# Output weights in 7168-byte runs, re-laid results and a one-row last load in a decode attention kernel

## The chip, the cores and the metric

One core of a Trainium2 chip. The core has a matrix engine (TensorE, PE in the profile), a vector engine (VectorE, DVE), a scalar engine (ScalarE, ACT), GpSimd (POOL) and SyncE (SP), which here only issues transfers. Sixteen DMA engines bring data from HBM to SBUF. Matmuls write to PSUM. The metric is the device time of one execution in microseconds (us); the profile's span runs from the first to the last instruction and is about 2 us shorter.

## The reference

One decode step of a block with attention and a dense part side by side, in bf16, for B = 2 rows of D = 448:

```python
xn = layernorm(x)
# A: 16 query heads, 8 KV heads (rep = 2), Dh = 256, the last W = 4096 keys of 32768
q = xn @ wq                                   # [2, 448] @ [448, 4096]
scores = q . k[:, :, Sk-W:, :] * Dh**-0.5
o = softmax(scores) @ v[:, :, Sk-W:, :]
a = o.reshape(2, 4096) @ wo                   # wo is [4096, 448]
# B: mish MLP
h = xn @ w1 + b1                              # F = 1792
b = (h * tanh(softplus(h))) @ w2
out = x + a + b
```

What has to be read is 2 x 8 x 4096 x 256 keys and as many values in bf16 (67.1 MB), and 3.67 MB each of wq and wo, and 1.6 MB each of w1 and w2: 77.66 MB in all.

## The kernel before

**Tiling.** The eight KV heads are worked off in U = 4 units. Unit u takes heads u and u + 4 of both batch rows, so J = 4 streams of 4096 keys. A unit's keys come in four loads of 2 MB (`load_k(u, r)`, L90, 16 KB per partition) and its values in four of 2 MB (`load_v(u, g)`, L96). Keys sit in a pool of 3 buffers, values in a ring of 4 (L67, L68). The query weights and w1 pass through the values' ring, w2 through a key buffer.

**One unit** (loop at L511). VectorE turns the keys of each load (`turns`, L498, two transposes at L243). When all four are turned, TensorE makes the scores in two halves (`scores`, L305), ScalarE the exponentials, VectorE turns them back (L333), and `weigh` (L340) sums them. Then `values` (L357) multiplies each tile of V; `gather` (L376) copies the result to SBUF and folds it by fp32 products with the masks `sel`, and `finish` (L409) divides by the sums. It leaves `oT`: the unit's attention output with the head dimension on the partitions, partition p holding rows 2p and 2p + 1 of each head's 256.

**Output product.** `load_wo(u)` (L105) brings the unit's part of wo, the 512 rows of each of its two KV heads (two query heads of 256), laid like `oT`: two rows of 448 to a partition, 1792 bytes per run, two loads of 448 KB. `mix` (L421) multiplies; `add_rows` (L221) splits the 448 output columns into G = 4 groups of 112 and puts each in another quarter of the PSUM tile `acc`, four matmuls for each row set. `mix(u - 1)` stands after `weigh(u)` in the unit loop. `acc` starts with x itself (L210 to L219) and takes all sums of attention and of the dense part.

**The end.** The last unit's fourth value tile is handled by `values_fixed` (L395), which works straight into the folded result, after `gather`. Then `finish`, `mix(3)`, and `dense_out` (L490) for the three loads of w2: all seven rows of the first half, five rows of the second, two rows of the second (`w2_parts`, L477). VectorE and ScalarE then copy `acc` into the result, and one store ends the kernel.

**Order.** The program is scheduled by hand: each engine works off its instructions in the order in which they are written, and SyncE issues all large loads in the written order. In a unit u below 3 that is V(u, 0) to V(u, 3), K(u + 1, 0) to K(u + 1, 2), wo(u), K(u + 1, 3); in the last unit wo(3), V, then w2. A load waits at SyncE until its buffer is free, and whatever is written after it waits behind it.

**PSUM.** Eight banks: two for scores, one each for the value products, the folded result, the sums and `acc`, and two (`ps_m`, L79) that rotate through the small products of the first stage (`xr_ps`, `q_ps`, `qt_ps`, `qr_ps`, `h_ps`).

Of the kernel before, what the change touches and what calls it, by code (L numbers as in the profile page):

```python
# [11 lines left out]
BF16 = mybir.dt.bfloat16  # L12
FP32 = mybir.dt.float32
PSUM = bass.MemoryType.PSUM
# [3 lines left out]
def kernel(  # L18
# [13 lines left out]
    nc = tc.nc  # L32
    P = 128
    G = 4
# [3 lines left out]
    Bsz, Sq, D = A_x.shape  # L38
    _, Hkv, Sk, Dh = A_k_cache.shape
    HqDh = A_wq.shape[1]  # L40
    Hq = HqDh // Dh
    rep = Hq // Hkv
# [3 lines left out]
    KU = J // Bsz  # L46
    U = Hkv // KU
# [11 lines left out]
    NI = F2 // P  # L59
    DG = D // G  # L60
# [11 lines left out]
    consts = ctx.enter_context(tc.tile_pool(name="consts", bufs=1))  # L72
    small = ctx.enter_context(tc.tile_pool(name="small", bufs=2))
# [2 lines left out]
    ps_o = ctx.enter_context(tc.tile_pool(name="ps_o", bufs=1, space=PSUM))  # L76
    ps_den = ctx.enter_context(tc.tile_pool(name="ps_den", bufs=1, space=PSUM))
    ps_a = ctx.enter_context(tc.tile_pool(name="ps_a", bufs=1, space=PSUM))
    ps_m = ctx.enter_context(tc.tile_pool(name="ps_m", bufs=2, space=PSUM))  # L79

    KE = T * Dh
    kview = A_k_cache.rearrange("b (k u) s d -> u (b k) s d", u=U)
# [5 lines left out]
    k_t, v_t, wo_t = {}, {}, {}  # L88

    def load_k(u, r):  # L90
        t = k_pool.tile([P, KE], BF16, tag="k", name="k")
        src = kview[u][:, s0:, :].rearrange("j (c t) d -> c j (t d)", c=C)
        nc.sync.dma_start(out=t[:], in_=src[:, :, r * KE : (r + 1) * KE])  # L93
        k_t[u, r] = t

    def load_v(u, g, lo=0, hi=T):  # L96
        if lo == 0:
            v_t[u, g] = ring("v")
        t = v_t[u, g]
        src = vview[u][:, s0:, :].rearrange("j (g x t) d -> g x j (t d)", g=G, x=C)  # L100
        nc.sync.dma_start(  # L101
            out=t[:, lo * Dh : hi * Dh], in_=src[g, :, :, lo * Dh : hi * Dh]
        )

    def load_wo(u):  # L105
        w = wo_pool.tile([P, KU, rep, 2 * D], BF16, tag="wo", name="wo")
        for k2 in range(KU):
            r0 = (u + U * k2) * rep * Dh
            nc.sync.dma_start(  # L109
                out=w[:, k2, :, :],  # L110
                in_=A_wo[r0 : r0 + rep * Dh, :].rearrange("(h p c) d -> p h (c d)", h=rep, p=P),
            )
        wo_t[u] = w

    x_bf = consts.tile([Bsz, D], BF16)
# [8 lines left out]
    for lo, hi in ((0, 4), (4, NS)):  # L124
# [5 lines left out]
    ident = consts.tile([P, P], BF16)  # L130
# [2 lines left out]
    nc.gpsimd.memset(qd[:], 0.0)  # L133
    ones = consts.tile([P, P], BF16)
    nc.gpsimd.memset(ones[:], 1.0)
    eps_t = consts.tile([Bsz, 1], FP32)
    nc.vector.memset(eps_t[:], 1e-5)

# [6 lines left out]
        out=rstd[:], in_=mv[:, 1:2], func=ACT.Sqrt, bias=eps_t[:], scale=1.0  # L145
# [4 lines left out]
        out=xn_bf[:],  # L150
# [8 lines left out]
        out=parm[:], in_=ident[:].rearrange("p (a o) -> p o a", o=2), axis=AXIS.X, op=ALU.add  # L159
# [3 lines left out]
        out=jm[:],  # L163
        in_=ident[:].rearrange("p (a j h) -> p j a h", j=J, h=rep),
# [4 lines left out]
        out=jm[:], in0=jm[:], scalar1=-1.0, scalar2=29952.0, op0=ALU.add, op1=ALU.mult  # L169
# [3 lines left out]
        out=mneg[:], in_=jm[:].unsqueeze(1).to_broadcast([P, TH * 8, J])  # L173
    )
    sel = consts.tile([P, 2, NQ], FP32)
    for x in range(2):
        for w in range(4):
# [4 lines left out]
            else:  # L182
                nc.vector.tensor_tensor(
                    out=sel[:, x, :], in0=sel[:, x, :], in1=src, op=ALU.add
                )

    xr_ps = ps_m.tile([P, NS, Bsz], BF16, tag="m", name="xr_ps")
    xn_v = xn_bf[:].rearrange("b (a k) -> b a k", k=NS)
    for s in range(NS):
        r = s // 2  # L190
        step = 3 + s % 2
        xrow = consts.tile([Bsz, P // 2, 2], BF16, name=f"xrow{s}")
        nc.vector.tensor_copy(out=xrow[:], in_=xn_v[:, :, r : r + step + 1 : step])  # L193
        nc.tensor.transpose(  # L194
            xr_ps[:, s, :], xrow[:].rearrange("b a o -> b (a o)"), ident[0:Bsz, 0:Bsz]
        )
    xs = consts.tile([P, NS, 32], BF16)
    nc.gpsimd.memset(xs[:], 0.0)
    for odd in range(2):
        for half in range(2):  # L200
            o = (half + odd) % 2
            nc.vector.tensor_scalar(
                out=xs[:, odd::2, half * Bsz : (half + 1) * Bsz],
# [3 lines left out]
                op0=ALU.mult,  # L207
            )

    acc = ps_a.tile([P, DG], FP32)  # L210
    for g in range(G):
        nc.tensor.matmul(
            acc[32 * g : 32 * (g + 1), :],
            lhsT=ident[0:Bsz, 0:32],
            rhs=x_bf[:, g * DG : (g + 1) * DG],
            start=True,
            stop=False,
            skip_group_check=True,
        )  # L219

    def add_rows(lhsT, rows, stop=False):  # L221
        for g in range(G):
            nc.tensor.matmul(  # L223
                acc[32 * g : 32 * g + Bsz, :],
                lhsT=lhsT,
                rhs=rows[:, g * DG : (g + 1) * DG],
                start=False,
                stop=stop,
                skip_group_check=True,
            )  # L230
# [20 lines left out]
    for n in range(2):  # L251
        for e in range(2):
            o = n * 64 + e
            sp = consts.tile([P, G, 32], BF16, name=f"sp{n}{e}")
            nc.gpsimd.tensor_copy(
                out=sp[:],
                in_=ident[:, o : o + 63 : 2].unsqueeze(1).to_broadcast([P, G, 32]),
# [47 lines left out]
    def scores(u, i):  # L305
        sc = ps_sc.tile([P, TH, 32], FP32, tag="sc", name="sc")
        nc.tensor.matmul(  # L307
            sc[:].rearrange("p t m -> p (t m)"),
            lhsT=ident[:],
            rhs=mneg[:].rearrange("p a j -> p (a j)"),  # L310
            start=True,
            stop=False,
            skip_group_check=True,
        )
        for n in range(NB):
            for e in range(2):
                for w in range(4):
                    nc.tensor.matmul(  # L318
                        sc[32 * w : 32 * (w + 1), :, :],
                        lhsT=qd[:, u, 2 * n + e, :, :].rearrange("p g q -> p (g q)"),  # L320
                        rhs=ktm[i][:, n, e, :, 32 * w : 32 * (w + 1)],
                        start=False,
                        stop=(n == NB - 1 and e == 1),
                        skip_group_check=True,
                    )
        ex = small.tile([P, TH, 32], BF16, tag="ex", name="ex")
        nc.scalar.activation(  # L327
            out=ex[:].rearrange("p t m -> p (t m)"),
            in_=sc[:].rearrange("p t m -> p (t m)"),
            func=ACT.Exp,  # L330
            scale=scale,
        )
        nc.vector.transpose(  # L333
            out=p_t[i][:].rearrange("p g t q -> p t g q"),
            in_=ex[:].rearrange("p t (g q) -> p t g q", g=G),
        )

    state = {}
# [70 lines left out]
    def finish(u):  # L409
# [8 lines left out]
        )  # L418
        state["oT", u] = oT

    def mix(u):  # L421
        oT, w = state.pop(("oT", u)), wo_t.pop(u)
        for k2 in range(KU):
            for h in range(rep):
                for c in range(2):
                    add_rows(oT[:, c, k2 * rep + h, :], w[:, k2, h, c * D : (c + 1) * D])
# [47 lines left out]
        nc.vector.tensor_tensor(out=t_sb[:], in0=t_sb[:], in1=den[:], op=ALU.mult)  # L474
        nc.vector.tensor_tensor(out=act_bf[:], in0=h_sb[:], in1=t_sb[:], op=ALU.mult)

    w2_parts = ((0, 0, NI), (1, 0, 5), (1, 5, NI))  # L477

    def load_w2(part):
        if part == 0:  # L480
            state["w2"] = k_pool.tile([P, KE], BF16, tag="k", name="w2")
        k, lo, hi = w2_parts[part]
        w2_in = B_w2.flatten().rearrange("(k p e) -> k p e", k=2, p=P)
        at = k * NI * D
        nc.sync.dma_start(
            out=state["w2"][:, at + lo * D : at + hi * D],
            in_=w2_in[k, :, lo * D : hi * D],
        )

    def dense_out(part):  # L490
        k, lo, hi = w2_parts[part]
        for i in range(lo, hi):
            at = (k * NI + i) * D
            add_rows(
                act_bf[:, i, k, :], state["w2"][:, at : at + D], stop=(k == 1 and i == NI - 1)
            )

    def turns(u, r):  # L498
        for i in range(NH):
            turn(u, r, i)  # L500
# [10 lines left out]
    for u in range(U):  # L511
        last = u == U - 1
        if last:
            load_wo(u)
        load_v(u, 0)
        load_v(u, 1)
        load_v(u, 2)
        if last:
            load_v(u, 3, 0, 24)
            load_v(u, 3, 24, T)  # L520
            for part in range(3):
                load_w2(part)
        else:
            load_v(u, 3)
            load_k(u + 1, 0)
            load_k(u + 1, 1)
            load_k(u + 1, 2)
            load_wo(u)
            load_k(u + 1, 3)
        scores(u, 0)  # L530
        scores(u, 1)
        weigh(u)
        if u > 0:
            mix(u - 1)
        for g in range(G - 1):
            values(u, g)
        if not last:
            values(u, G - 1)
            turns(u + 1, 0)
            turns(u + 1, 1)  # L540
            gather(u)
            finish(u)
            turns(u + 1, 2)
            turns(u + 1, 3)
    u = U - 1
    gather(u, last=False)
    values_fixed(u, G - 1, 0, 24)
    values_fixed(u, G - 1, 24, T)
    finish(u)
    mix(u)  # L550
    for part in range(3):
        dense_out(part)

    res = consts.tile([Bsz, D], BF16)
# [38 lines left out]
```

The softmax here doesn't subtract the row's maximum and nothing guards it: scores larger than these inputs give would overflow.

## Time and profile before

| | |
|---|---|
| time, median of 3 | 193.05 us (192.83 to 193.07) |
| span of the profiled execution | 191.1 us |
| bytes moved | 77.80 MB, 77.66 of them on SyncE's queue |
| DVE busy | 90.7 us (47%) |
| PE busy | 69.5 us (36%), weight loads 33.6 |
| ACT busy, POOL busy | 11.3 us, 2.9 us |
| wo loads | 8 of 448 KB |
| w2 loads | 784 KB, 560 KB, 224 KB |

The busy shares are averages over the whole span. The slices cut the span into 40 equal parts: a digit is the busy share of one part in tenths (9 is 90% or more), "DMA" is the mean over the sixteen DMA engines, and "GB/s" is what they moved. The queue list gives packets, megabytes and the share of sixteen engines' span. The chain follows the work that ended last back from the end. In a line of the timeline the columns are start, length, engine, line, operation, output<-inputs, shapes and count, and in brackets the idle time before it with what ended it; consecutive instructions of one kind are merged. Matmul lengths are modelled and overlap.

### The profile page before, as it was taken

How to read it: one execution, taken by the hardware profiler on the slowest of the kernel's cores; microseconds unless marked ns; L12 is line 12 of the kernel's file. 1: busy time of each engine (PE TensorE's matmuls, PEld its weight loads, DVE VectorE, ACT ScalarE, POOL GpSimd, SP SyncE). 2: the span in 40 equal slices, each digit the busy share in tenths (PEclk: the TensorE clock that was granted, in tenths of full speed). 3: DMA queues.
4: the chain of work that ended last, by engine and by line, in shares of the span. 5: the costliest groups of instructions: out<-in, count | busy, mean ns of one | idle time of the engine just before them, and what ended most of it. 6: DMA issues, size and time to landing. Idle time of an engine off the chain costs nothing.

```text
span 191.1 us, 2051 instructions
## 1 busy us (share of the span) xinstructions
PE 69.5 (36%) x892; PEld 33.6 (18%) x892; DVE 90.7 (47%) x96; ACT 11.3 (6%) x19; POOL 2.9 (2%) x13
## 2 busy tenths in 40 slices
PE   0201525197236000097334000395262000674492
PEld 0100115032104000033113000132031000222191
DVE  4887066583001998543004995823007994731001
ACT  3000030011001000011000000010010000020101
POOL 6000000000000000000000000000000000000000
PEclk9999999999955555559955555579855555599655
DMA  5999999999999999999999999999999999999980
GB/s 216 408 419 423 434 421 449 415 429 425 435 432 422 425 404 424 435 435 422 418 429 432 435 408 415 429 425 432 432 429 418 415 421 404 436 418 425 414 351 19
DMA packets 8081, 77.80 MB, mean 407 GB/s; under 512 B 1028, under 2 KB 3208, under 8 KB 3592
## 3 DMA queue, kind: packets, MB, share of 16 engines
q1 hardware_dynamic: 7796, 77.66, 96.7%
q8 instruction: 7, 0.11, 0.2%
q10 hardware_dynamic: 276, 0.01, 0.1%
q14 instruction: 2, 0.02, 0.0%
HBM read 77.67 MB, written 0.00 MB: 406 GB/s over the span
## 4 chain that ended last, share of the span: by engine, by line
DMA 86%; DVE 7%; SPq 2%; PE 2%; issue 0%; DVEq 0%
DMA k<-in_A_k_cache_dram 53%; DMA w<-in_B_w_dram 27%; DVE kt L243 7%; DMA wo<-in_A_wo_dram 7%; PE h_ps L443 1%; SPq L93 1%; SPq L126 1%; PE acc L223 0%; SPq L101 0%; DVEq L588 0%; DVE res L559 0%; SPq L109 0%
## 5 line engine op out<-in xcount | busy, mean ns | idle before, releaser
L243 DVE STREAM_TRANSPOSE kt<-k 128x2048 f32<-128x2048 f32 x32 | 72.1, 2291 | 55.4 <-DMA k<-in_A_k_cache_dram 55.4
L318 PE MATMUL sc<-kt,qd 128*32 128x512 bf16 x256 | 23.2, 519 | 62.2 <-DVE kt L243 62.2
L365 PE MATMUL pv<-v,p 128*32 128x512 bf16 x240 | 19.2, 456 | 23.1 <-DMA v<-in_A_v_cache_dram 23.1
L318 PEld LDWEIGHTS <-qd 128*32 128x32 bf16 x256 | 8.6, 117 | 74.6 <-issue 72.4
L365 PEld LDWEIGHTS <-p 128*32 128x32 bf16 x240 | 7.0, 106 | 33.5 <-issue 29.9
L333 DVE STREAM_TRANSPOSE p<-ex 128x512 bf16<-128x512 bf16 x8 | 5.7, 711 | 14.5 <-ACT ex L327 14.5
L327 ACT ACTIVATE ex<-sc 128x512 bf16<-128x512 f32 x8 | 4.8, 598 | 85.4 <-PE sc L318 85.4
L385 PE MATMUL o<-sel,vs 128*128 128x8 f32 x32 | 7.5, 364 | 2.9 <-ACT vs L379 2.9
L385 PEld LDWEIGHTS o<-sel,vs 128*128 128x128 f32 x32 | 7.1, 325 | 6.5 <-ACT vs L379 6.5
L265 PE MATMUL q_ps<-wq,xs 128*32 128x512 bf16 x28 | 3.4, 623 | 12.5 <-DMA wq<-in_A_wq_dram 12.5
L412 DVE TENSOR_TENSOR oT<-o,rec 128x16 bf16<-128x16 f32 x4 | 0.6, 145 | 12.2 <-PE o L400 12.2
L379 ACT COPY vs<-pv 128x512 f32<-128x512 f32 x4 | 2.3, 586 | 48.2 <-PE pv L365 48.2
L343 PE MATMUL dn<-p,ones 128*128 128x512 bf16 x8 | 3.1, 383 | 4.5 <-DVE p L333 4.5
L443 PE MATMUL h_ps<-xs,w 128*128 128x4 bf16 x49 | 2.8, 193 | 5.1 <-DMA w<-in_B_w_dram 5.1
L307 PE MATMUL sc<-mneg,ident 128*128 128x512 bf16 x8 | 4.6, 571 | 0.0
L282 DVE COPY qT<-qt_ps 128x16 bf16<-128x16 bf16 x4 | 0.4, 168 | 6.9 <-PE qt_ps L277 6.9
L351 DVE TENSOR_REDUCE rec<-dn 128x8 f32<-128x512 f32 x4 | 2.8, 692 | 1.9 <-PE dn L343 1.9
L443 PEld LDWEIGHTS <-w 128*128 128x128 bf16 x49 | 2.7, 152 | 5.2 <-DMA w<-in_B_w_dram 5.2
L265 PEld LDWEIGHTS <-xs 128*32 128x32 bf16 x28 | 1.1, 125 | 14.0 <-issue 14.0
L194 PE MATMUL xr_ps<-ident,xrow 2*128 2x2 bf16 x7 | 1.0, 181 | 6.5 <-DVE xrow L193 6.5
L223 PEld LDWEIGHTS <-oT 128*2 128x2 bf16 x128 | 1.8, 91 | 5.5 <-issue 5.1
L223 PE MATMUL acc<-wo,oT 128*2 128x112 bf16 x128 | 2.6, 232 | 0.3 <-DVE oT L412 0.3
(51 smaller groups left out, 28.8 us busy)
## 6 DMA issues: line engine op xcount, KB each, us to landing
k<-in_A_k_cache_dram SPq DMA_DIRECT2D x16, 2048.0 KB, 27.1
v<-in_A_v_cache_dram SPq DMA_DIRECT2D x15, 2048.0 KB, 23.6
wo<-in_A_wo_dram SPq DMA_DIRECT2D x8, 448.0 KB, 30.5
wq<-in_A_wq_dram SPq DMA_DIRECT2D x1, 2048.0 KB, 16.3
w<-in_B_w_dram SPq DMA_DIRECT2D x1, 1568.0 KB, 26.9
wq<-in_A_wq_dram SPq DMA_DIRECT2D x1, 1536.0 KB, 19.3
v<-in_A_v_cache_dram SPq DMA_DIRECT2D x1, 1536.0 KB, 26.8
w<-in_B_w_dram SPq DMA_DIRECT2D x1, 784.0 KB, 23.9
```

The lines of the kernel that those rows point to most:

```text
L223: nc.tensor.matmul(acc[32 * g : 32 * g + Bsz, :], lhsT=lhsT, rhs=rows[:, g * DG : (g + 1) * DG], start=False, stop=stop, skip_group_check= ...
L243: nc.vector.transpose(out=kt[i][:, :, :, r, :], in_=t[:, i * w : (i + 1) * w].bitcast(FP32).rearrange("p (a c j) -> p a c j", c=P // (R * ...
L265: nc.tensor.matmul(q_ps[32 * u : 32 * (u + 1), :], lhsT=xs[:, s, :], rhs=wq_t[s][:, u * 512 : (u + 1) * 512], start=(s == 0), stop=(s == N ...
L307: nc.tensor.matmul(sc[:].rearrange("p t m -> p (t m)"), lhsT=ident[:], rhs=mneg[:].rearrange("p a j -> p (a j)"), start=True, stop=False, ...
L318: nc.tensor.matmul(sc[32 * w : 32 * (w + 1), :, :], lhsT=qd[:, u, 2 * n + e, :, :].rearrange("p g q -> p (g q)"), rhs=ktm[i][:, n, e, :, 3 ...
L327: nc.scalar.activation(out=ex[:].rearrange("p t m -> p (t m)"), in_=sc[:].rearrange("p t m -> p (t m)"), func=ACT.Exp, scale=scale,)
L333: nc.vector.transpose(out=p_t[i][:].rearrange("p g t q -> p t g q"), in_=ex[:].rearrange("p t (g q) -> p t g q", g=G),)
L343: nc.tensor.matmul(dn[:].rearrange("p a q -> p (a q)"), lhsT=ones[:], rhs=p_t[i][:].rearrange("p g t q -> p (g t q)"), start=(i == 0), sto ...
L351: nc.vector.tensor_reduce(out=rec[:], in_=dn[:].rearrange("p a q -> p q a"), axis=AXIS.X, op=ALU.add)
L365: nc.tensor.matmul(pv[32 * w : 32 * (w + 1), :, :].rearrange("p x d -> p (x d)"), lhsT=p_t[a // 4][:, g, 4 * (a % 4) : 4 * (a % 4) + 4, :] ...
L385: nc.tensor.matmul(po[:, c, :], lhsT=sb[:, x, c::2], rhs=sel[:, x, :], start=(x == 0 and c == 0), stop=(last and x == 1), skip_group_check ...
L443: nc.tensor.matmul(h_ps[:, i, :, :].rearrange("p k b -> p (k b)"), lhsT=w1_v[:, s, i, :], rhs=xs[:, s, 0 : 2 * Bsz], start=(s == 0), stop= ...
```

## The change

**Three units' output weights in longer runs.** For units 0 to 2, eight consecutive rows of wo go to one partition: 8 x 448 x 2 = 7168 bytes in one run, 128 runs, one load of 896 KB. Row y * 8 + i of KV head k lies at partition (y, k), place i. That is no longer the layout of `oT`.

**Re-laid results.** So `relay` brings `oT` into the new layout by products with one-hot masks (`hot`, made at the start on GpSimd): 16 small matmuls pick for each partition its rows, and ScalarE copies the result to `ox`.

**Mixed at full width, ahead of the next scores.** `mix_early` multiplies `ox` by the weights in eight matmuls of all 448 columns into a new PSUM tile `early`, in place of 32 matmuls of 112 columns into `acc`. Both stand ahead of `scores` of the next unit instead of after `weigh`. `early` starts with x. In the last unit `carry` copies `early` to SBUF and puts it into `acc` by four fp32 products with a 2 x 2 identity; the last unit itself is mixed as before. `early` has its own bank, so `ps_m` falls from two to one. The seven small rows `xrow` move into buffers that the exponentials use later.

**Last load one row.** The second half of w2 comes in 4 + 2 + 1 rows instead of 5 + 2.

```diff
-    ps_m = ctx.enter_context(tc.tile_pool(name="ps_m", bufs=2, space=PSUM))
+    ps_e = ctx.enter_context(tc.tile_pool(name="ps_e", bufs=1, space=PSUM))
+    ps_m = ctx.enter_context(tc.tile_pool(name="ps_m", bufs=1, space=PSUM))
...
     def load_wo(u):
         w = wo_pool.tile([P, KU, rep, 2 * D], BF16, tag="wo", name="wo")
-        for k2 in range(KU):
+        if u < U - 1:
+            nc.sync.dma_start(
+                out=w[:].rearrange("p k h e -> p (k h e)"),
+                in_=A_wo.rearrange("(k u y i) d -> u y k (i d)", k=KU, u=U, i=8)[u],
+            )
+        for k2 in range(KU if u == U - 1 else 0):
...
+    id2 = consts.tile([Bsz, Bsz], FP32)
+    nc.vector.tensor_copy(out=id2[:], in_=ident[0:Bsz, 0:Bsz])
+    hot = consts.tile([P, KU, 4, 32, KU], BF16)
+    nc.gpsimd.memset(hot[:], 0.0)
+    for k in range(KU):
+        nc.gpsimd.tensor_copy(
+            out=hot[:, k, :, :, k], in_=ident[:].rearrange("p (q y) -> p y q", y=4)
+        )
...
+    early = ps_e.tile([Bsz, D], FP32)
+    nc.tensor.matmul(
+        early[:], lhsT=ident[0:Bsz, 0:Bsz], rhs=x_bf[:], start=True, stop=False
+    )
     acc = ps_a.tile([P, DG], FP32)
-    for g in range(G):
-        nc.tensor.matmul(
-            acc[32 * g : 32 * (g + 1), :],
...
+    def carry():
+        e_sb = small.tile([P, 2 * Dh], FP32, tag="vs", name="e_sb", bufs=1)[0:Bsz, 0:D]
+        nc.scalar.copy(out=e_sb, in_=early[:])
+        for g in range(G):
+            nc.tensor.matmul(
+                acc[32 * g : 32 * g + Bsz, :],
+                lhsT=id2[:],
+                rhs=e_sb[:, g * DG : (g + 1) * DG],
+                start=True,
...
+    def relay(u):
+        oT = state.pop(("oT", u))
+        ox_ps = ps_m.tile([P, 4, 2, Bsz], FP32, tag="m", name="ox_ps")
+        for h in range(rep):
+            rows = slice(h * 64, (h + 1) * 64)
+            for y in range(4):
+                for k in range(KU):
+                    nc.tensor.matmul(
+                        ox_ps[rows, y, :, :],
+                        lhsT=hot[:, k, y, :, :].rearrange("p q k -> p (q k)"),
+                        rhs=oT[:, :, k * rep + h, :],
...
+        nc.scalar.copy(
+            out=ox[:].rearrange("p i b -> p (i b)"),
+            in_=ox_ps[:].rearrange("p y c b -> p (y c b)"),
+        )
...
+    def mix_early(u):
+        ox = state.pop(("ox", u))
+        w = wo_t.pop(u)[:].rearrange("p k h (c d) -> p (k h c) d", c=2)
+        for i in range(8):
+            nc.tensor.matmul(
+                early[:],
+                lhsT=ox[:, i, :],
+                rhs=w[:, i, :],
...
-    w2_parts = ((0, 0, NI), (1, 0, 5), (1, 5, NI))
+    w2_parts = ((0, 0, NI), (1, 0, 4), (1, 4, 6), (1, 6, NI))
...
+        if u > 0:
+            relay(u - 1)
+            mix_early(u - 1)
+        if last:
+            carry()
         scores(u, 0)
         scores(u, 1)
         weigh(u)
-        if u > 0:
-            mix(u - 1)
```

## The prediction

> **What bounds the kernel now.** I read the page first: the busy shares, the slices, the queues, the chain.
>
> ```profile
> span 191.1 us, 2051 instructions
> PE 69.5 (36%) x892; PEld 33.6 (18%) x892; DVE 90.7 (47%) x96; ACT 11.3 (6%) x19; POOL 2.9 (2%) x13
> ...
> DMA  5999999999999999999999999999999999999980
> GB/s 216 408 419 423 434 421 449 415 429 425 435 432 422 425 404 424 435 435 422 418 429 432 435 408 415 429 425 432 432 429 418 415 421 404 436 418 425 414 351 19
> DMA packets 8081, 77.80 MB, mean 407 GB/s; under 512 B 1028, under 2 KB 3208, under 8 KB 3592
> ...
> q1 hardware_dynamic: 7796, 77.66, 96.7%
> q8 instruction: 7, 0.11, 0.2%
> ...
> DMA 86%; DVE 7%; SPq 2%; PE 2%; issue 0%; DVEq 0%
> ```
>
> No compute engine is busy for half the span, while the DMA row is full from the second slice to the last but one. So the 77.66 MB are one unbroken stream, and the time is head + bytes/rate + tail. The 7% of DVE in the chain are turns after which SyncE may issue the next key load. They don't drain the queue: a key load takes 27.1 us from issue to landing (the page's list of issues), so there is always work ahead. The thinnest place I found is 65.83 us, when K(1,3) is issued: behind K(1,0), which landed at 61.3, some 5.1 MB were queued, of which 4.5 us at 0.43 MB/us removed 2; about 7 us were left.
>
> The rate is not flat. Adding up the trace's packet records by microsecond gives 426 to 430 GB/s for most of the span, but 404, 383, 395, 418 in 69 to 73 us, and the same dent at 111 to 115, 152 to 156 and 159 to 163: one for each unit's output weights. The same records by size:
>
> ```
> size B   packets   mean ns of one   GB/s of 16 engines
>  1792      2176        77.6             369
>  4480       128       173.2             414
>  6272       128       245.4             409
> 12288       256       462.0             426
> 16384      4096       617.4             425
>     4       754         9.1             (one per engine and transfer: its semaphore)
> ```
>
> Then the end, in order of time.
>
> ```profile
> 178.77 1.90 PE L365 MATMUL pv<-v,p 128*32 128x512 bf16 x16 [3.85 <-DMA v<-in_A_v_cache_dram]
> ...
> 180.77 0.59 ACT L379 COPY vs<-pv 128x512 f32<-128x512 f32 x1 [10.06 <-PE pv L365]
> ...
> 181.41 1.87 PE L385 MATMUL o<-sel,vs 128*128 128x8 f32 x8 [0.74 <-ACT vs L379]
> ...
> 183.13 1.85 PE L400 MATMUL o<-p,v 128*128 128x8 bf16 x64
> 185.02 0.17 DVE L412 TENSOR_TENSOR oT<-o,rec 128x16 bf16<-128x16 f32 x1 [12.17 <-PE o L400]
> ...
> 185.25 0.92 PE L223 MATMUL acc<-wo,oT 128*2 128x112 bf16 x32 [0.27 <-DVE oT L412]
> ...
> 185.95 0.87 PE L223 MATMUL acc<-w,act_bf 128*2 128x112 bf16 x28
> 186.97 0.92 PE L223 MATMUL acc<-w,act_bf 128*2 128x112 bf16 x28 [0.15 <-DMA w<-in_B_w_dram]
> ```
>
> From the third value tile (landed 178.73) TensorE runs nearly without a gap, and two clocks end together. TensorE would reach the second w2 part at 186.83; that part landed at 186.93, hence the wait of 0.15. The single records in the last group show another stop of about 0.13 us, before its last eight matmuls (187.30 to 187.53): they wait for the last load, whose packets end at 187.07. I put that landing at 187.49. So DMA ends last, by a little, and TensorE's tail stands 0.1 to 0.3 us behind it. Taking DMA time out pays fully, because the value tiles that start TensorE's tail move with it.
>
> [...] The trace agrees: a line through 1792 B (77.6 ns) and 16384 B (617.4) has 0.0370 ns per byte and 11.3 ns left at zero bytes. [...]
>
> **The change part by part.**
>
> *Output weights of units 0 to 2.* A unit's 917,504 B came in 512 packets of 1792 B, 512 x 77.6 / 16 = 2.48 us of every engine. Now they are 128 packets of 7168 B. None is in the trace; by the line above one takes 277 ns, so 128 x 277 / 16 = 2.22 us. Saved: 0.27 us a unit, 0.80 for three; half as many semaphore packets, -0.03. Bounds: the dents alone are 0.11 MB short of 428 GB/s, 0.26 us a unit, of which the overhead that 7168 B still has (about 0.04) stays: 0.22, or 0.66 for three. If 7168 B ran without overhead (0.9175 MB at 428 GB/s, 2.14 us): 0.34, or 1.02.
>
> *Last load of one row.* The seven rows of w2's second half came as 5+2 and now come as 4+2+1. Per group of three runs: 3584 B (144 ns by the line) + 1792 (77.6) + 896 (44) = 266 against 173.2 + 77.6 = 251; 8 per engine, +0.12 us with the semaphore. In exchange, four matmuls instead of eight stand behind the last landing. Those eight start in two fours 0.048 us apart, so that gains 0.05, and the 0.15 us wait goes as well, since the four-row part lands 0.26 us earlier.
>
> *Relay, early mix, carry.* Per unit 16 matmuls of 4 columns with a weight load each, one small ACT copy, 8 matmuls of 448 columns; out go 32 of 112 columns (0.56 us in 89.17 to 89.73, between the softmax sums and the values). No row shows the new shapes. From below: 448 columns at full clock, 0.19 us x 8 = 1.5. From above: at half clock the score groups pass 512 columns in 0.43 us, so 448 take 0.37, x 8 = 3.0; L443's 49 loads and matmuls in 2.77 us put the 16 at 0.9; copy and hand-overs 0.5. I take 4.4 us. They stand ahead of the scores, where TensorE idles: "PE sc <- DVE kt" shows 62.2 us over four times, 19.4 before each of units 1 to 3. They need the unit's oT (70.62 for unit 0, 153.89 for unit 2), and its weights, queued ahead of the fourth key load: about 157 for unit 2. From there only the 8 matmuls remain, to about 160.5; the carry adds an ACT copy (0.59, from the 512-wide row) and four fp32 matmuls that I bound by 1.8 from L385's rows: 163. The scores start at 164.04, so it fits by a microsecond. If not, unit 3's values have 3.85 us of waiting on V to absorb it. Cost on the path: 0.
>
> *Waits added.* With one buffer in the small PSUM pool, h_ps must wait for the qd copies: these end at 27.4, h_ps starts at 30.75 on a landing. The relay waits for oT, the copy for the relay; behind the copy on ACT stands only the next exponential, 10 us later. The hot masks are 1 to 2 us of POOL by 3.5 us (L255: 0.3 each); xs, then zeroed, is first needed at 7.65. All zero.
>
> *Sum.* Stream: -0.80 - 0.03 + 0.12 = -0.71. Behind it: -0.05. TensorE's own tail: starts 0.83 earlier, reaches w2's second half at 186.0, needs 0.65 us, so it is also done in time. Total -0.76: 193.05 - 0.76 = 192.29.
>
> **The rivals.** *Absorbed, 192.9* (chance 0.10). The last landing is that of the slowest engine; the last packets of the sixteen spread over 185.0 to 187.07. If the slowest lags from something else, such as the instruction queue's seven 16 KB fetches (1.04 to 1.11 us each, at 182.5 and 186.8 too), less packet overhead may not show. Against: every engine carries the same share of small packets. *Slower, 193.8* (0.06). Two interleaved halves of the matrix, 7168 B at a time, might read worse: at the worst dent's 383 GB/s all through, 0.9175 MB take 2.40, no gain, and the split adds 0.12; or late weights push the scores of the last unit past their slack. I would then see +0.1 to +0.8. Against: the key loads read in the same interleaved form at 425. *More, 191.8* (0.12). 7168 B without overhead (-1.02), and the fetches fall behind the last load instead of beside it, or the end comes at full clock (0.2).
>
> **How the numbers follow.** The forecast (-0.66 to -0.95 in the stream, around 192.3) has 0.72. Range 191.8 to 192.8: it takes in both bounds of the packet price and most of "more", and leaves out the slower case and half of the absorbed one. Faster by over 0.2% means under 192.66: forecast and "more", 0.83; within 0.2%: 0.11; slower: 0.06.
>
> **What would show it.** The packets under 2 KB fall by about 1440 (1536 gone, 128 of 896 B come, 32 fewer for semaphores), q1's count by about 1056, and the dents at 69 and 111 us vanish while that at 159 stays. A 7168 B packet takes 270 to 285 ns. The early mix sits inside the idle time before the scores, and these still wait for the turns. At the end the wait on w2 is gone, and four matmuls follow the last landing. Wrong would be: a packet over 310 ns; a DMA row with a hole; scores that wait for the mix; a last landing that hasn't moved.

## The result and the profile after

The changed kernel takes 192.27 us (192.14 to 192.48, 4 executions) against 193.0; the ratio is 0.9964, interval [0.9947, 0.9982]. A later set gave 192.54 against 193.17, again 0.9962 [0.9950, 0.9973]. The forecast was 192.29. Its total was met, but the sum behind it was not, and most of what follows is about that.

The head of the page after the change:

```profile
span 190.1 us, 2021 instructions
PE 79.8 (42%) x873; PEld 37.8 (20%) x873; DVE 91.5 (48%) x97; ACT 12.3 (6%) x23; POOL 4.0 (2%) x16
...
GB/s 221 390 435 427 442 418 434 424 422 428 428 431 428 421 427 425 431 434 424 424 428 428 434 421 428 428 431 421 438 424 421 422 433 400 434 428 418 416 377 29
DMA packets 7025, 77.79 MB, mean 409 GB/s; under 512 B 997, under 2 KB 1769, under 8 KB 2537
...
q1 hardware_dynamic: 6740, 77.66, 96.8%
q8 instruction: 6, 0.10, 0.2%
```

The same bytes come in 1056 fewer packets on SyncE's queue, 1439 fewer under 2 KB. By size, a 7168 B packet takes 275.4 ns (the prediction's line gave 277), one of 3584 B 140, one of 896 B 41. Added up by microsecond, the dents at 69 and 111 us are gone (421 GB/s or more where 383 and 388 stood) and the one of the last unit, whose weights came as before, is still there (390 at 160 us). One line will matter later: the instruction queue (q8) has 6 packets of 16 KB in place of 7.

The relay, the early mix and the carry sit where they were expected. The timeline before the last unit's scores:

```profile
153.57 0.14 DVE L436 TENSOR_TENSOR oT<-o,rec 128x16 bf16<-128x16 f32 x1
153.76 0.78 PE L452 MATMUL ox_ps<-oT,hot 128*64 128x4 bf16 x16 [9.87 <-DVE oT L436]
...
156.24 3.14 PE L471 MATMUL early<-wo,ox 128*2 128x448 bf16 x8 [1.71 <-DMA wo<-in_A_wo_dram]
...
159.48 0.52 ACT L234 COPY e_sb<-early 2x448 f32<-2x448 f32 x1 [4.73 <-PE early L471]
160.05 0.37 PE L236 MATMUL acc<-e_sb,id 2*2 2x112 f32 x8 [0.67 <-ACT e_sb L234]
...
163.49 3.21 PE L342 MATMUL sc<-kt,qd 128*32 128x512 bf16 x32 [2.75 <-DVE kt L267]
```

The mix waits 1.71 us for its weights, as foreseen, and the scores still wait for the turns afterwards (2.75 us). The end of the program:

```profile
178.22 1.90 PE L389 MATMUL pv<-v,p 128*32 128x512 bf16 x16 [2.99 <-DMA v<-in_A_v_cache_dram]
...
184.70 0.91 PE L247 MATMUL acc<-wo,oT 128*2 128x112 bf16 x32 [0.27 <-DVE oT L436]
...
185.40 2.04 PE L247 MATMUL acc<-w,act_bf 128*2 128x112 bf16 x56
186.99 0.18 PEld L247 LDWEIGHTS <-act_bf 128*2 128x2 bf16 x11 [0.48 <-issue]
187.43 0.56 DVE L620 CAST res<-acc 2x112 bf16<-2x112 f32 x2 [2.78 <-PE acc L247]
...
188.05 0.34 SPq L623 DMA_DIRECT2D out_dram<-res  x1
```

Put beside the trace before, in us (a load has landed when the last of its sixteen engines has signalled):

```
                                   before    after   difference
last load landed                   187.49   186.95     -0.54
result copies start                187.91   187.43     -0.48
store issued                       188.55   188.05     -0.50
store landed                       189.71   189.22     -0.49
end of the span                    191.15   190.09     -1.06
device time minus span (median)      1.80     2.05     +0.25
```

So only half a microsecond comes from the stream of loads. Another 0.57 comes after the store has landed, where the change does nothing that it was meant to do, and 0.25 is given back outside the span. (The profiled execution before had 1.92 there; the medians of four sets of its executions, 118 in all, are 1.77 to 1.80.) These were the questions for the experiments.

### The profile page after: what moved, and what is told of

Read it like the earlier page. It is cut to its first block, busy times and chain, and to the rows that moved or that the text cites. A ratio compares the mean times of both kernels' runs of the same rounds, so it can differ in the third digit from the quotient of the medians.

```text
span 190.1 us, 2021 instructions
## 1 busy us (share of the span) xinstructions
PE 79.8 (42%) x873; PEld 37.8 (20%) x873; DVE 91.5 (48%) x97; ACT 12.3 (6%) x23; POOL 4.0 (2%) x16
## 4 chain that ended last, share of the span: by engine, by line
DMA 85%; DVE 10%; issue 3%; SPq 1%; PE 0%; DVEq 0%
DMA k<-in_A_k_cache_dram 66%; DMA w<-in_B_w_dram 12%; DVE kt L267 10%; DMA wo<-in_A_wo_dram 7%; PE acc L247 0%; SPq L115 0%; SPq L94 0%; DVEq L649 0%; DVE res L620 0%; DVE oT L436 0%
## 5 line engine op out<-in xcount | busy, mean ns | idle before, releaser
L342 PE MATMUL sc<-kt,qd 128*32 128x512 bf16 x256 | 22.0, 500 | 13.9 <-DVE kt L267 13.9
L452 PE MATMUL ox_ps<-oT,hot 128*64 128x4 bf16 x48 | 2.3, 192 | 29.7 <-DVE oT L436 29.7
L471 PE MATMUL early<-wo,ox 128*2 128x448 bf16 x24 | 9.4, 571 | 5.1 <-DMA wo<-in_A_wo_dram 5.1
L452 PEld LDWEIGHTS <-hot 128*64 128x64 bf16 x48 | 2.5, 151 | 29.6 <-issue 29.5
L471 PEld LDWEIGHTS <-ox 128*2 128x2 bf16 x24 | 2.8, 115 | 9.6 <-issue 8.5
L331 PE MATMUL sc<-mneg,ident 128*128 128x512 bf16 x8 | 4.1, 514 | 0.0
L210 PE MATMUL xr_ps<-ident,xrows 2*128 2x2 bf16 x7 | 1.0, 180 | 6.6 <-DVE xrows L209 6.6
```

The source lines that it names most:

```text
L331: nc.tensor.matmul(sc[:].rearrange("p t m -> p (t m)"), lhsT=ident[:], rhs=mneg[:].rearrange("p a j -> p (a j)"), start=True, stop=False, ...
L342: nc.tensor.matmul(sc[32 * w : 32 * (w + 1), :, :], lhsT=qd[:, u, 2 * n + e, :, :].rearrange("p g q -> p (g q)"), rhs=ktm[i][:, n, e, :, 3 ...
L452: nc.tensor.matmul(ox_ps[rows, y, :, :], lhsT=hot[:, k, y, :, :].rearrange("p q k -> p (q k)"), rhs=oT[:, :, k * rep + h, :], start=(y == ...
L471: nc.tensor.matmul(early[:], lhsT=ox[:, i, :], rhs=w[:, i, :], start=False, stop=(u == U - 2 and i == 7),)
```

## The experiments

The expectations stand as they were written before each run, and name several theories. The stream theory: the gain is all in the loads' cheaper packets. The end theory, of the first four runs: besides that, the store's place in the order of SyncE's last waits pays; later this is the order theory. The stall theory, with which I ended and which I call the list theory: an engine stands still at a fixed place of its instruction list, and the change moved SyncE's place into a harmless wait and TensorE's into the tail. Two more rivals: the last load of one row is what pays; the mix ahead of the scores is what pays.

At the end SyncE waits in both traces for its transfers' completion counters, two per instruction in five instructions, and then closes the program. These are its instructions of the program's end, from 189.75 us on, in the trace before, where the store landed at 189.71. The columns are line, engine and operation, count, shortest/median/longest ns, start of the first and last. EVENT_SEMAPHORE is a wait or a signal; three short DRAIN instructions among them have a line of their own, which is left out here and below.

```profile
L588 SPq EVENT_SEMAPHORE  x5: 17/28/28, 190.2 to 191.1; - x5
```

The same from 189.75 us on in the trace after the change, where the store landed at 189.22:

```profile
L649 SPq EVENT_SEMAPHORE  x1: 17/17/17, 190.0 to 190.0; - x1
```

Before, the first of the five that are left starts at 190.2 (190.16), after a stop of 0.44 us in which nothing runs on SyncE. The store's counter is in the second of the five instructions there. After the change it is in the fifth and last, no stop follows it, and by 189.75 only the very last one is left.

**Long runs with 5 + 2 rows**, the changed kernel without the split of the last load.

```diff
-    w2_parts = ((0, 0, NI), (1, 0, 4), (1, 4, 6), (1, 6, NI))
+    w2_parts = ((0, 0, NI), (1, 0, 5), (1, 5, NI))
```

> The changed kernel with w2's second half back at 5 + 2 rows. Stream theory (the gain is the cheaper packets of three units' output weights, 0.22 us each in the trace, 0.66 in all, and the one-row last load costs about 0.1): 192.3 against 193.0 before, at or just under the changed kernel. End theory (some 0.5 us of the gain come after the store, because at the end SyncE waits for the transfers' completion counters in a fixed order and the store's counter, second in that order before, is last after the change; here it is last but one): about 0.5 below the stream theory's figure, 191.8 to 191.9. Rival (the one-row last load is what pays): 192.6 or more.

Measured: 192.90, ratio 0.9989 [0.9982, 0.9995]. Neither figure: by the ratios half a microsecond slower than the changed kernel, though its stream is as fast (last landing 187.11, with a start that was 0.13 later). With 47 transfers in place of 48 SyncE's stop is back, 189.71 to 190.13, now behind all five waits and so exposed. And TensorE has a stop of its own, in the timeline of this kernel's tail (PEld are the weight loads; the page after the change has 873 of them and 873 matmuls):

```profile
186.59 0.62 PE L247 MATMUL acc<-w,act_bf 128*2 128x112 bf16 x17 [0.16 <-DMA w<-in_B_w_dram]
...
187.41 0.18 PEld L247 LDWEIGHTS <-act_bf 128*2 128x2 bf16 x11 [0.46 <-issue]
```

The last eight matmuls could have started when the last load landed, at 187.11; instead the last eleven start at 187.41, and the idle time is put down to "issue", which means that the profile shows nothing that the engine waited for. The same x11 stands in the tail of the changed kernel above.

**The one-row last load alone**, on the kernel before.

```diff
-    w2_parts = ((0, 0, NI), (1, 0, 5), (1, 5, NI))
+    w2_parts = ((0, 0, NI), (1, 0, 4), (1, 4, 6), (1, 6, NI))
...
```

> The kernel before with only w2's second half in 4 + 2 + 1 rows. Stream theory: 128 more packets, +0.1, and less than 0.1 back from fewer matmuls behind the last landing: 193.0 to 193.1. End theory: the store's counter falls into the first pair that SyncE waits for, as good as second: the same 193.0 to 193.1. Rival (the one-row last load pays): 192.6 to 192.8.

Measured: 193.07 against 193.07, 0.9999 [0.9991, 1.0007]. The last landing is at 187.65, 0.16 later than before, but the third value tile, ahead of all parts of w2, had already landed 0.17 later (178.90 against 178.73). So this trace shows no cost of the split in the stream. From the last landing to the first copy of the result it takes 0.33 us where it took 0.43, and the whole gives nothing. SyncE's stop moved one wait forward, directly behind the first.

**Changed kernel with short runs.** Everything as changed, but the same layout of the weights read in 1792 B runs.

```diff
-            nc.sync.dma_start(
-                out=w[:].rearrange("p k h e -> p (k h e)"),
-                in_=A_wo.rearrange("(k u y i) d -> u y k (i d)", k=KU, u=U, i=8)[u],
-            )
+            for i2 in range(4):
+                nc.sync.dma_start(
+                    out=w[:, i2 // 2, i2 % 2, :],
+                    in_=A_wo.rearrange("(k u y j i) d -> u j y k (i d)", k=KU, u=U, j=4, i=2)[u, i2],
+                )
```

> The changed kernel (relay, mix ahead of the scores, carry, 4 + 2 + 1) with the same layout of the three units' weights read in 1792-byte runs, four loads of 224 KB a unit in place of one of 896 KB: 512 packets a unit, as before. Stream theory: the 0.66 us are lost again, the dents in the stream at 69 and 111 us are back, and the split's 0.1 stays: 193.0 to 193.1. End theory: the store's counter is third in order, so its 0.5 us is lost too: 193.0 to 193.2. Rival (the gain comes from the mix being ahead of the scores, not from the run length): 192.3.

Measured: 193.05, 0.9998 [0.9990, 1.0006]. So no gain of the mix ahead of the scores shows. But I had the end wrong: with 57 transfers there was no stop of SyncE behind the store. What took its place was the longest stop of TensorE in any run, again ahead of the last eleven; its timeline:

```profile
186.15 1.54 PE L248 MATMUL acc<-w,act_bf 128*2 128x112 bf16 x45
188.24 0.18 PEld L248 LDWEIGHTS <-act_bf 128*2 128x2 bf16 x11 [1.00 <-issue]
```

The last load had landed at 187.67, so 0.57 us are lost. The comparison is spoiled as a measure of the run length; it is made again below.

**The kernel before, six spare loads.**

```diff
             for part in range(3):
                 load_w2(part)
+            for t in range(6):
+                spare = consts.tile([Bsz, 16], BF16, name=f"spare{t}")
+                nc.sync.dma_start(out=spare[:], in_=A_x.flatten_outer_dims()[:, 0:16])
```

> The kernel before with six spare loads of 64 bytes (never read) behind the w2 loads, so that the store's completion counter is the last in SyncE's order at the end, as in the changed kernel; nothing else differs. Stream theory alone: 193.0, no change. End theory: 192.4 to 192.5, with the last matmul where it was (187.9 us in the trace) and the span after the store's issue 2.0 us in place of 2.6.

Measured: 192.37 against 193.07, 0.9962 [0.9949, 0.9974]. Six loads that nobody reads give the kernel before the same 0.7 us that the whole change gives. In its trace the last load lands no earlier (187.74), and the store goes out at 188.79; the span then ends 1.96 us later, at 190.7, where before it took 2.59. SyncE's instructions from 189.75 us on, in this kernel:

```profile
L591 SPq EVENT_SEMAPHORE  x3: 17/17/28, 189.9 to 190.7; - x3
```

The first of the three is the last of the five waits, over just behind the landing of the store (189.92).

**The kernel before, two spare loads**, to tell the order of the waits from the stop.

```diff
...
+            for t in range(2):
...
```

> The kernel before with two spare loads of 64 bytes (never read) behind the w2 loads, where six gave 192.37. With two, the store's counter falls into the first pair that SyncE waits for at the end, as with the one-row load alone (193.07). Order theory (the last place among the waits is what pays): 193.1. Stall theory (SyncE stands still for about 0.44 us at one fixed place of its instruction list; before, that place falls behind the wait for the store, and each further load moves it one wait forward, until it lies in front of that wait and is hidden in it): 192.6, and no stop after the store has landed.

Measured: 192.76, 0.9984 [0.9977, 0.9990]. The order theory alone can't be it: the store's counter is in the first pair and the time still falls. The stop is gone. SyncE's instructions from 189.75 us on, in this kernel:

```profile
L591 SPq EVENT_SEMAPHORE  x7: 17/28/28, 190.0 to 191.0; - x7
```

The store landed at 189.97, the first wait is over at 189.99, and the other four follow 0.07 to 0.08 apart. The gain is 0.32 and not 0.44, and the other 0.39 to the six-load version are the waits that still follow (four of 0.07), with 0.1 left over. So both count, the stop and the store's place in the order. In the traces with 47, 48, 50 and 51 transfers the stop falls behind the fifth wait, into the fifth wait (hidden, because that is the one for the store), behind the second and behind the first; with 52 it is ahead of all. So one transfer more moves it forward by one place, as it would if it were fixed in SyncE's list (49 were not tried).

**Both lists put right**: long runs, 5 + 2 rows, one spare load (48 transfers), and nineteen idle matmuls at the start, the number by which the change had shortened TensorE's list.

```diff
     early = ps_e.tile([Bsz, D], FP32)
+    for _ in range(19):
+        nc.tensor.matmul(
+            early[:, 0:8], lhsT=ident[0:Bsz, 0:Bsz], rhs=x_bf[:, 0:8], start=True, stop=True
+        )
```

> The changed kernel with w2 back at 5 + 2 rows, one spare load of 64 bytes (48 transfers again, as in the changed kernel) and 19 small idle matmuls at the start, so that TensorE's instruction list is as long as before. Stall theory for both engines (TensorE too stands still at a fixed place of its list, eleven matmuls ahead of the end in the three traces with the relay; 19 more instructions push that place back to where it was before, ahead of the landing of w2): last matmul at 187.2 us in place of 187.55 with 5 + 2 rows alone, no stop after the store, 192.0 to 192.1. If TensorE's stop is a late landing and no stall of its own: 192.4 to 192.5.

Measured: 191.91, 0.9935 [0.9922, 0.9947]. The kernel does more work and is 0.6% faster than the kernel before. The last matmuls start at 187.08, 0.1 behind the landing at 186.98; the page shows seven instruction packets again, and the device time is 1.81 above the span.

**Its counterpart with short runs**, 56 transfers, everything else alike.

> The counterpart of the run just named: relay, early mix and carry, 5 + 2 rows, 19 idle matmuls, but the three units' weights in 1792-byte runs (four loads of 224 KB a unit; 56 transfers, where SyncE's stall is hidden too). The two differ in the run length alone. Stream theory: 0.6 to 0.7 us slower than it, 192.6 to 192.8. If longer runs give nothing at the end of the kernel: the same.

Measured: 192.48, 0.9970 [0.9959, 0.9982]. This is the clean price of the run length: 0.57 us by the medians, 0.68 by the two ratios. The dents are back; comparing the times at which the two traces have moved the same number of bytes, each of the three units costs 0.22 to 0.24. The same run bears on the price of the relay, the mix and the carry: it has all three with short runs, and is 0.11 us above the kernel before with six spare loads (192.37), with intervals that overlap.

**Only the start of the change** on the kernel before: masks, identity, moved small rows.

```diff
+    hot = consts.tile([P, KU, 4, 32, KU], BF16)
+    nc.gpsimd.memset(hot[:], 0.0)
+    ...
```

> The kernel before with only the start of the changed one: the one-hot masks on GpSimd, the 2 x 2 identity and the moved small rows, none of them used later. In all runs with the relay the device time is 2.05 us above the span, in those without it 1.80. If this comes from the work added at the start: 193.3, with the span as before. If not: 193.07.

Measured: 193.24 against 193.08, but the ratio is 1.0001 [0.9993, 1.0009], and the device time is 1.81 above the span. The quarter microsecond doesn't come from there. The two medians are 0.16 apart, but the interval of the ratio takes in 1, so a difference is not shown.

**The changed kernel again**, for the two beside it.

> The changed kernel itself, on the same chip as the next two and with more executions than the four it has. 192.2 to 192.4 (192.27 before), with the device time 2.05 us above the span.

Measured: 192.54, 0.9962 [0.9950, 0.9973], 2.03 above the span. The profiled one is 192.61. In it the last load landed at 187.13, 0.36 earlier than before, but TensorE's stop ahead of the last eleven matmuls lasted to 187.49:

```profile
187.49 0.18 PEld L247 LDWEIGHTS <-act_bf 128*2 128x2 bf16 x11 [0.80 <-issue]
187.92 0.56 DVE L620 CAST res<-acc 2x112 bf16<-2x112 f32 x2 [3.08 <-PE acc L247]
```

In the trace before, the copy of the result starts at the same time:

```profile
187.91 0.56 DVE L559 CAST res<-acc 2x112 bf16<-2x112 f32 x2 [2.72 <-PE acc L223]
```

So in this execution nothing of what the loads gained reached the result; its span is shorter (190.6 against 191.1) only by what comes after the store was issued. From the last landing to the first copy it takes 0.43 us in the kernel before. It takes 0.33 where only four matmuls follow the landing and no stop stands in the way (the one-row load alone, and the next run), 0.48 in the first profile of the changed kernel, and 0.79 here. Against 0.33 the stop costs 0.15 and 0.46. Two profiles can't show that this makes the spread of the changed kernel's executions (192.13 to 192.61), but it is of that size.

**The changed kernel with nineteen idle matmuls** and nothing else.

> The changed kernel with only the 19 small idle matmuls at the start, which make TensorE's list as long as before. From the sum so far: the 0.25 us outside the span go (2.05 to 1.80 above it) and so does TensorE's stop of about 0.1 near the end: 191.9 to 192.0, the same as the version with 5 + 2 rows (191.91) or up to 0.1 above it. If the 5 + 2 rows and not the longer list had made that one faster: 192.3.

Measured: 191.77, 0.9928 [0.9916, 0.9940]: 0.77 faster than the changed kernel beside it, for work that is thrown away. The time above the span is 1.79. The idle matmuls don't do it through TensorE's clock: from 182 to 187.4 us the granted clock is 0.50, half of the full one, in this trace and in that of the changed kernel beside it. The timeline of its tail, which now waits for landings only:

```profile
185.19 2.10 PE L251 MATMUL acc<-w,act_bf 128*2 128x112 bf16 x56
186.19 0.36 PEld L251 LDWEIGHTS <-act_bf 128*2 128x2 bf16 x16 [0.31 <-issue]
186.80 0.32 PEld L251 LDWEIGHTS <-act_bf 128*2 128x2 bf16 x11 [0.25 <-issue]
187.32 0.56 DVE L624 CAST res<-acc 2x112 bf16<-2x112 f32 x2 [2.89 <-PE acc L251]
```

The two groups of loads start at the landings of the four-row part (186.15) and of the two-row part (186.75), and the last four matmuls at 187.03, 0.04 behind the last landing. A "x11" stands here too, but by the landing and not by the list: the bracket can't tell the two apart, the landing times can.

Neither stop delays the end here, nor in the kernel before with six spare loads (0.9962). So the distance of these two is what the change is worth by itself: 0.66 us by the ratios, 0.60 by the medians, close to the 0.57 to 0.68 of the run length.

**The changed kernel with two spare loads.**

> The changed kernel with only two spare loads of 64 bytes (never read) behind the w2 loads: 50 transfers, as many as in the kernel before, so that SyncE's stop falls behind the landing of the store again and three more waits follow it. All else as changed. Stall theory: 0.55 to 0.65 us slower than the changed kernel, 192.8 to 192.9. If the end of SyncE's list has no part in the changed kernel's gain: 192.3.

Measured: 193.02, 0.9991 [0.9985, 0.9998]: 0.48 slower than the changed kernel beside it. With as many transfers as the kernel before, the change is worth 0.15 us. SyncE's instructions of the program's end from 189.75 us on, in this kernel:

```profile
L652 SPq EVENT_SEMAPHORE  x5: 17/28/28, 190.0 to 190.9; - x5
```

The store landed at 189.51; the next instruction of SyncE comes at 189.97, so the stop is back, with the same five instructions behind it as in the kernel before.

**The kernel before with a longer list**, 109 idle matmuls at the start. TensorE's stop lies eleven matmuls ahead of the end in the traces with 873 matmuls and is not seen with 892. In the trace before, the packets of 16 KB on the instruction queue start 127 matmuls apart in the mean. 892 + 109 are 1001, 128 more than 873: if the stop comes again at that distance, it lies at the same place here.

```diff
     acc = ps_a.tile([P, DG], FP32)
+    for _ in range(109):
+        nc.tensor.matmul(
+            acc[0:32, 0:8],
+            lhsT=ident[0:Bsz, 0:32],
+            rhs=x_bf[:, 0:8],
+            start=True,
+            stop=True,
+            skip_group_check=True,
+        )
```

> The kernel before with 109 small idle matmuls at the start, in time in which TensorE waits for wq; nothing else differs. [...] List theory (TensorE's stop and the quarter microsecond outside the span come from the length of its instruction list alone): a stop 11 matmuls ahead of the end, 2.3 to 2.6 us after the last such packet starts, 193.3 to 193.8. If both belong to the relay and the other added work: 193.1.

Measured: 193.48 against 193.13, 1.0022 [1.0014, 1.0031]. The device time is 2.07 above the span (2.00 to 2.09), where the executions of the kernel before have 1.73 to 1.96, and the trace has a stop from 187.41 to 187.53, eleven matmuls ahead of the end with 1001 matmuls as with 873: the two places are 128 matmuls apart. But the stop costs nothing here: the last load lands later still (187.60), and from there to the first copy it takes 0.43 as in the kernel before. Of the 0.35, 0.27 are outside the span. Both the stop and the time outside come without the relay.

The starts of the last 16 KB packet on the instruction queue beside the end of TensorE's stop:

```
                              packet starts   stop ends   apart   last load landed
changed kernel                       184.50      186.99    2.49             186.95
long runs, 5 + 2                     184.79      187.41    2.62             187.11
short runs                           185.92      188.24    2.32             187.67
changed kernel again                 185.21      187.49    2.28             187.13
changed, two spare loads             184.77      187.30    2.53             187.00
before, 109 more                     185.13      187.53    2.40             187.60
```

In the kernel before, and with nineteen more in the changed one, a packet starts at 182.5 and 181.7, and TensorE gets to that place of its list later than 2.6 us after it: in the kernel before the 863rd matmul starts at 186.51, 4.0 us after the packet. So in six traces the stop ends 2.28 to 2.62 us after the packet starts. That such a packet brings a part of TensorE's list, and that TensorE waits for it in the stop, is my estimate from the counts (6 packets within the span with 873 matmuls, 7 with 892), from this table, and from the distance of the packets: in the trace before, the seven start when 101 to 864 matmuls have started, 127 apart in the mean. No run shows what a packet holds.

## Why the prediction came out right, point by point

**What bounds the kernel**: right for the stream. It is unbroken, and most of the three units' saving arrives at the last landing (0.54 us in the first trace, of 0.66 by the bytes moved). That the last landing also sets the result holds in the trace before and not in those of the changed kernel, where TensorE's stop stands between the two (landed at 186.95 and 187.13, stop over at 186.99 and 187.49).

**Output weights, -0.80**: right in mechanism, the term too large. By bytes moved, the three units save 0.23, 0.22 and 0.21 in the trace, 0.66 in all; the matched pair gives 0.57 to 0.68. The price of a 7168 B packet was right within 2 ns. What failed was to take 512 x 77.6 / 16 as time: records of packets overlap a little, and the DMA share in the window of a dent (69 to 73 us before) is 1.07. The lower bound of the prediction, taken from the dents, was the right figure. The 11.3 ns at zero bytes are an estimate from two rows of the trace before, 1792 B and 16384 B; at 896 B, where their line gives 44 ns, a packet took 41. The new source's step of 7168 B did no harm that the 275.4 ns would show.

**Split of the last load, +0.12 in the stream, -0.05 behind it**: neither size is confirmed. The packets of 3584 B and 896 B were cheaper than the line said (140 and 41 ns for 144 and 44), which leaves 0.07 of the 0.12. At the last landing nothing of it can be seen. From the landing of the last value load to that of the last w2 load it is 3.80 us in the changed kernel and 3.81 with 5 + 2 rows, 3.81 in the kernel before and 3.81 with the one-row load. It is 3.95 with nineteen idle matmuls and the split, against 3.80 with 5 + 2 rows, but it also varies without any split: 4.14 in the kernel with only the masks. Behind the landing, four matmuls in place of eight give 0.10 where no stop stands in the way, twice the forecast. In the changed kernel they don't come: eleven matmuls follow the stop. As times, the split measures 0.9999 alone, and with nineteen idle matmuls the split version (191.77, 0.9928) and the 5 + 2 version (191.91, 0.9935) can't be told apart.

**Relay, mix and carry at zero**: right. They took 0.78 + 3.14 + 0.37 us on TensorE where 0.9 + 3.0 + up to 1.8 were assumed, and the scores wait for the turns behind them. The 3.14 us were at a mean granted clock of 0.52. The lower bound of 0.19 us for 448 columns follows from the trace before, where at a granted clock of 1.00 (168 to 170 us) groups of 512 columns start 0.22 us apart. Two kernels with short runs and no stop in the way, with them (192.48, 0.9970) and without (192.37, 0.9962), can't be told apart.

**The sum, -0.76**: it agrees with the measurement by cancellation, which is luck. What it should have held, from the first profile: -0.54 at the last landing, -0.10 behind it, +0.15 for TensorE's stop, -0.57 at the end of SyncE's list, +0.25 outside the span. That is -0.81; the medians give -0.73 and -0.63. The change by itself is worth 0.60 to 0.66, and what its two side effects on the lists add is not in the prediction. With two spare loads, and so as many transfers as before, the same change takes 193.02, above the 191.8 to 192.8 that the prediction gave. The step that failed is "Sum": it ended at the last matmul and took everything behind it, and everything outside the span, as unchanged. It also had TensorE "done in time" and no term for a wait of its own. The rival "more" named the instruction queue's fetches as something that might move (1.02 to 1.11 us each in the trace; the prediction reads 1.04 to 1.11), but as traffic beside the loads, not as something that TensorE's stop follows. Its end at full clock (0.2) is shown by no run: from 182 to 187.4 us the granted clock was 0.50 in the trace before and in that after the change.

**The signs to look for** all came but one: eleven matmuls, and not four, follow the last landing, and they wait for the stop to end.

## What to carry to other kernels

When a change of under half a percent moves the number of instructions or of transfers, its time has to be compared with list lengths held equal: a few idle matmuls or spare loads bring the counts back and show whether the gain belongs to the change. Read the trace past the last matmul to the end of the span, and take the device time minus the span as a row of its own. Runs of 1792 B cost 0.22 us per 0.9 MB here against runs of 7168 B, measured by bytes moved and not by adding up packet times.

## What the runs showed that I had not expected

SyncE stands still for about 0.44 us (0.44 in the trace before, 0.42 with 5 + 2 rows, 0.46 with two spare loads in the changed kernel) at what looks like one place of its list, and where that falls, with the store's place among the waits, decides over 0.3 to 0.7 us at the end. Its cause is not shown: no instruction packet falls into it, and the nearest, of 8 KB, starts 0.6 to 0.9 us after it has ended.

TensorE's stop stood in the tail of small matmuls, eleven ahead of the end, with 873 and with 1001 matmuls, and ended 2.28 to 2.62 us after a 16 KB packet had started. That the list comes in pieces of 128 matmuls with their weight loads is my estimate from the 128 between these two places and the 127 between packets. In six of the sets of executions the median of the device time is 2.03 to 2.07 us above the span, in the others 1.77 to 1.81; two of the six, of 13 and 22 executions, have one at 1.81 and 1.76. The six are just those whose trace has no instruction packet in the last 2 us before the result (186.2 to 187.3 in the others). What costs the 0.25 us there is not shown; that it follows the length of TensorE's list is shown by the nineteen idle matmuls (1.79 us in place of 2.03) and the 109 (2.07 in place of 1.80).

The sixteen engines drift apart, mostly at one place, and stay apart: a load's first and last engine land 0.56 us apart at 30.7 us (30.15 and 30.71), and 1.78 apart at 41.7, after an instruction packet at 36.0; at the end it is 2.0. Each load thus lands late by what its slowest engine lags. What drives them apart was not tested.
